# Rotary embedding on GpSimd cut into nine instructions, and two small steps moved, in an attention and gated-convolution kernel

## Chip, core and metric

The kernel runs on one core of one Trainium2 chip. The metric is device time in microseconds (us) for one execution, from launch to end; times stand as the median of three executions. The engines are TensorE (PE in the profile, with PEld for its weight loads), VectorE (DVE), ScalarE (ACT), GpSimd (POOL) and SyncE (SP), whose queue issues the DMAs here.

## Reference

Attention with a rotary embedding (rope) on q and k, then two matrix products with a three-tap convolution and a gate between them. All arrays are f32.

```python
batch, n_heads, seq, head_dim = 4, 8, 576, 64      # d_model 512, d_ff 1024
def rotate(x):                                      # half = 32
    x1, x2 = x[..., :half], x[..., half:]
    return concat([x1 * cos - x2 * sin, x1 * sin + x2 * cos])
scores = rotate(q) @ rotate(k).T / sqrt(64)
attn = softmax(scores)                              # row maximum subtracted
x = (attn @ v) laid out as (batch, seq, 512)
h = relu(x @ w_in)
c = conv_w[0] * h[t-1] + conv_w[1] * h[t] + conv_w[2] * h[t+1]
out = (h * sigmoid(c)) @ w_out
```

## The kernel before

The work on attention goes by pairs of heads, p = 0 to 15, with five score tiles each (`emit_S`, steps s = 0 to 4). A hand-written plan puts every piece into a numbered slot n with a rank; within a slot, pieces are emitted by rising rank, and each engine runs its instructions in the order of emission. Pair p has its score tiles in slots 5p to 5p+4. Up to slot 25 (`WIDE` is 26) the kernel does attention and turns the weights from 64-bit to f32 (`conv_w_piece`, lines 469 to 530); the text calls this the attention stage. From slot 26 on, the matrix products of the second part (`emit_M1`, `emit_M2`) are woven in between; this is the mixed stage. A tail runs the last two blocks of the second part alone.

For one score tile PE writes scores to PSUM (line 232), DVE takes the negated row maximum (`reds`, line 240), ACT takes the exponential with the row sum (`exps`, line 244), PE transposes the result (lines 289, 301 and 306), and ACT or DVE copies it out to `pt` (`evac`, lines 170 and 172). Two score tiles fit into PSUM, so PE's next scores wait for ACT's exponential to free one. `emit_Trem` makes the small transposes and their copies, and `emit_E` multiplies the probabilities by v (line 342); its last products read the small copies.

Rope of pair p runs on POOL (lines 163 and 164): one multiplication over 1152 columns in place, and one addition over 576 columns. It is emitted at the end of slot 5p-6 for q and 5p-5 for k. DVE turns the results by a 32x32 transpose into `qT` and `kT` (`emit_TQ`, lines 209 and 213) in slots 5p-4 and 5p-2. After the q transpose, ACT multiplies `qT` by the scale in place (line 210, recorded under the helper's line 170). That multiplication goes through `defer(k, ...)`: it is emitted k ticks later, a tick being one step of a piece on PE, of which a slot has some four to six.

`emit_rinv` (lines 315 and 316, DVE) adds a small number to the row sums and takes reciprocals; `emit_rinvT` a slot later turns them with PE and spreads them by DMA; `norm` uses them three slots after `emit_rinv`.

The second part's DVE work for one block of 128 features is lines 385 (multiply), 387 twice (multiply and add), and 396 (gate), all from SBUF; ACT and POOL split the result into two parts (lines 404 and 405). POOL also splits the normalized attention output (line 359).

Of the kernel before, what the change touches and what calls it, by code (L numbers as in the profile page):

```python
# [12 lines left out]
ALU = mybir.AluOpType  # L13
# [7 lines left out]
def attention_moe_kernel(ctx, tc, q, k, v, w_in, conv_w, w_out, tab, tabx, out):  # L21
    nc = tc.nc
# [12 lines left out]
    scale = float(D) ** -0.5  # L35
# [21 lines left out]
    tabt = keep.tile([128, S // 32, 2, 32], F32, name="tabt")  # L57
# [21 lines left out]
    def defer(k, fn, rank=1):  # L79
        due.setdefault(slot[0] + k, []).append((rank, len(due.get(slot[0] + k, [])), fn))  # L80
# [79 lines left out]

    def rope(p, part):
        x = raw[p, part]
        nc.gpsimd.tensor_tensor(out=x, in0=x, in1=tabt, op=ALU.mult)  # L163
        nc.gpsimd.tensor_tensor(out=x[:, :, 0, :], in0=x[:, :, 0, :], in1=x[:, :, 1, :], op=ALU.add)

    QT, KT = {}, {}

    def evac(eng, out, in_, sc=None):
        if eng == "A" or "m" not in psum:
            nc.scalar.activation(out=out, in_=in_, func=AF.Copy, scale=1.0 if sc is None else sc)  # L170
        elif sc is None:
            nc.vector.tensor_copy(out, in_)
        else:
            nc.vector.tensor_scalar(out=out, in0=in_, scalar1=sc, scalar2=None, op0=ALU.mult)

    def qk_tiles(p):
        if p not in QT:
            QT[p] = p2.tile([128, S], F32, tag="qT", name="qT")
            KT[p] = p2.tile([128, S + 64], F32, tag="kT", name="kT")

    def k_rem(p):
        if p * STEPS < WIDE:
            for h in range(2):
                r = slice(64 * h, 64 * h + 64)
                evac("V", krem[p % 2][r, r], KT[p][r, 576:640])
# [19 lines left out]
    def emit_TQ(p, part):  # L205
        qk_tiles(p)
        x = raw.pop((p, part))[:, :, 0, :]
        if part == "q":
            nc.vector.transpose(out=QT[p].rearrange("p (c i) -> p c i", i=32), in_=x)
            defer(1, lambda: evac("A", QT[p], QT[p], scale))  # L210
        else:
            kt = KT[p].rearrange("p (c i) -> p c i", i=32)
            nc.vector.transpose(out=kt[:, 2:20], in_=x)
            nc.vector.transpose(out=kt[:, 0:2], in_=x[:, 16:18])
            k_rem(p)
# [5 lines left out]
    def go(d, key):  # L221
        for fn in d.pop(key):
            fn()
# [58 lines left out]
    def emit_T(p, s, h=None):  # L282
        if p not in PT:
            PT[p] = ptp.tile([128, 9, S], F32, tag="pt", name="pt")
        pt = PT[p]
        ps = t_tile()
        st = STR[p] if s == 4 else ST[p, s][:, h, 64 * h:64 * h + 512]
        for t in range(4):
            nc.tensor.transpose(ps[:, 128 * t:128 * t + 128], st[:, 128 * t:128 * t + 128], idf)  # L289
        if s == 4:  # L290
            evac("A", pt[:, 0:8, 512:S], ps.rearrange("p (k c) -> p k c", k=8))
        else:
            evac("A", pt[:, h:8:2, 128 * s:128 * s + 128], ps.rearrange("p (k c) -> p k c", k=4))

    def emit_Trem(p, g):
        pt = PT[p]
        ps = t_tile()
        if g < 2:
            for u in range(2):
                x = ST[p, 2 * g + u].rearrange("p h k -> p (h k)")[:, 512:640]  # L300
                nc.tensor.transpose(ps[:, 128 * u:128 * u + 128], x, idf)
            evac("V", pt[:, 8, 256 * g:256 * g + 256], ps[:, 0:256])
        else:
            for h in range(2):
                x = strem[p % 2][:, 512 - 64 * h:640 - 64 * h]
                nc.tensor.transpose(ps[:, 128 * h:128 * h + 128], x, idf)
            for h in range(2):
                r = slice(64 * h, 64 * h + 64)
                evac("V", pt[r, 8, 512:S], ps[r, 192 * h:192 * h + 64])
# [3 lines left out]
    def emit_rinv(p):  # L313
        s = p % 2
        nc.vector.tensor_scalar(out=sums[p], in0=sums[p], scalar1=1e-9, scalar2=None, op0=ALU.add)
        nc.vector.reciprocal(out=rvc[s][:, 0:9], in_=sums[p])

    def emit_rinvT(p):
        s = p % 2
        ps = t_tile()[0:32, 0:128]  # L320
        nc.tensor.transpose(ps, rvc[s], idf)
        st = p1.tile([32, 128], F32, tag="rst", name="rst")
        evac("V", st, ps)
        d = scr.tile([9, 128], F32, tag="d", name="rd")
        nc.sync.dma_start(out=d, in_=st[0:9, :])
        fl = d.rearrange("(o t) n -> o (t n)", o=1)
        rbt = rb[p] = p1.tile([128, S], F32, tag="rb", name="rb")
        nc.sync.dma_start(out=rbt[0:64, :], in_=fl[:, 0:S].to_broadcast([64, S]))
        nc.sync.dma_start(out=rbt[64:128, 0:512], in_=fl[:, 640:1152].to_broadcast([64, 512]))
        nc.sync.dma_start(out=rbt[64:128, 512:S], in_=fl[:, 576:640].to_broadcast([64, 64]))  # L330
# [5 lines left out]
    def emit_E(p, j):  # L336
        b, hp = divmod(p, NPB)
        xp = t_tile()
        o = (S - XW) * j
        for i in range(5):  # L340
            for h in range(2):
                nc.tensor.matmul(  # L342
                    out=xp[64 * h:64 * h + 64, 0:XW],
                    lhsT=vmain[p][:, h, i, :] if i < 4 else vrem[:, h, :],
                    rhs=PT[p][:, 2 * i + h if i < 4 else 8, o:o + XW],
                    start=(i == 0),
                    stop=(i == 4),
                )
        xn = p2.tile([128, XW], F32, tag="xn", name="xn", bufs=3)
        nc.scalar.activation(out=xn, in_=xp[:, 0:XW], func=AF.Copy)  # L350

        def norm():
            sl = xslot[b, hp, j] = free_slots.pop(0)
            nc.vector.tensor_tensor(out=xn, in0=xn, in1=rb[p][:, o:o + XW], op=ALU.mult)

        def split():
            sl = xslot[b, hp, j]
            nc.scalar.activation(out=xT[:, sl, 0, :], in_=xn, func=AF.Copy)  # L358
            nc.gpsimd.tensor_tensor(out=xT[:, sl, 1, :], in0=xn, in1=xT[:, sl, 0, :].bitcast(F32), op=ALU.subtract)  # L359

        norms[p, j] = lambda: (norm(), defer(1, split))
# [208 lines left out]
    def at(n, rank, fn):  # L570
        plan.setdefault(n, []).append((rank, len(plan.get(n, [])), fn))

    def emit():
        with tc.manual_schedule(engines=engines):
# [17 lines left out]
            for p in range(1, NP):  # L592
                n = STEPS * p
                for i, part in enumerate("qk"):
                    if p > 1:
                        at(n - 9 + 2 * i, 19, lambda p=p, part=part: load(p, part))
                    at(max(n - 6 + i, 0) if p > 1 else 0, 18, lambda p=p, part=part: rope(p, part))
                    at(max(n - 4 + 2 * i, 2), 0.45, lambda p=p, part=part: emit_TQ(p, part))
                at(n + 1, 19, lambda p=p: load_v(p))
            for p in range(NP):  # L600
                n = STEPS * p
                for s in range(STEPS):
                    m = n + s
                    first = m < WIDE
                    if m:
                        at(m - 1 if first else m, 0.5 if first else 0, lambda p=p, s=s: emit_S(p, s))
                    at(m, 0.2, lambda p=p, s=s: go(reds, (p, s)))
                    at(m, 0.3 if first else 1.5, lambda p=p, s=s: go(exps, (p, s)))
                    for h in range(2 if s < 4 else 1):
                        at(m + 1, 0 if m + 1 < WIDE else 1, lambda p=p, s=s, h=h: emit_T(p, s, h))  # L610
                for g, e in ((0, 2), (1, 4), (2, 5)):
                    at(n + e, 2, lambda p=p, g=g: emit_Trem(p, g))
                at(n + 4, 4, lambda p=p: emit_E(p, 0))
                at(n + 5, 4, lambda p=p: emit_E(p, 1))
                at(n + 5, 1.7, lambda p=p: emit_rinv(p))
                at(n + 6, 2, lambda p=p: emit_rinvT(p))
                for j in range(2):
                    at(n + 8, 1.7 + j, lambda p=p, j=j: norms.pop((p, j))())
            nw = len(wsteps)
            for i, u in enumerate(wsteps):  # L620
                x = (WIDE - 1) * i // nw
# [66 lines left out]
            for u in seq + second + m2_units(last) + m2_units(LASTB):  # L688
                u()
                tick()  # L690

    emit()


# [47 lines left out]
```

## Time and profile before

| What | Value |
|---|---|
| Median of three executions | 581.32 us (576.83 to 585.36) |
| Profiled execution, its own time | 585.31 us |
| Span of the profiled execution, first to last instruction | 583.2 us |
| PE busy | 513.9 us, 88% of the span |
| DVE busy | 417.5 us, 72% |
| ACT busy | 316.6 us, 54% |
| POOL busy | 241.3 us, 41% |
| Granted TensorE clock, mean | 0.959 of full speed |

A busy share says how long an engine had something in it, also while that instruction waited inside the engine. The chain of waits ends last through PE for 58% of the span, through DVE for 21% and through ACT for 9%. What a stretch is worth is read from the idle time of PE in it and from who ended that idle time.

### The profile page before, as it was taken

To read this page: it belongs to the slowest core of one execution; us is meant where nothing else is said; L and a number is where in the kernel's file an instruction comes from. 1 tells how busy PE (TensorE), PEld (TensorE's weight loads), DVE (VectorE), ACT (ScalarE), POOL (GpSimd) and SP (SyncE) were. 2 spreads that over 40 slices of the span, in tenths; PEclk is the share of its full clock that TensorE was granted. 3 is DMA by queue.
4 is the path that set the end of the run, shared out by engine and by line. 5 is a ranking of instruction groups with operands and counts; after the bars stand their busy time and mean duration, and the time that the engine had idled before them with its cause. 6 is when DMAs were issued, how large, how long until landed. Compare 5 with 4: busy or idle time off the path is not lost.

```text
span 583.2 us, 9069 instructions
## 1 busy us (share of the span) xinstructions
PE 513.9 (88%) x3160; PEld 364.0 (62%) x3160; DVE 417.5 (72%) x668; ACT 316.6 (54%) x810; POOL 241.3 (41%) x221
## 2 busy tenths in 40 slices
PE   3597879788895999897998899997998999999997
PEld 1253434344664667674777577674866767779986
DVE  4888778784586958878598848877288847466971
ACT  2678676675654655565546545574255646334530
POOL 3636547554363534427071714545044212142440
PEclk9979989998896999999999989997999999999999
DMA  9774663934422315051513214060240101000001
GB/s 216 138 155 117 150 143 90 197 75 82 81 42 57 67 50 92 8 113 22 113 28 83 59 54 88 17 124 1 77 83 21 41 22 39 22 37 19 1 36 55
DMA packets 138385, 42.51 MB, mean 73 GB/s; under 512 B 131004, under 2 KB 131940, under 8 KB 138340
## 3 DMA queue, kind: packets, MB, share of 16 engines
q1 hardware_dynamic: 136996, 41.54, 32.6%
q8 instruction: 25, 0.41, 0.3%
q10 hardware_dynamic: 1344, 0.39, 0.3%
q14 instruction: 20, 0.16, 0.1%
HBM read 37.12 MB, written 4.79 MB: 72 GB/s over the span
## 4 chain that ended last, share of the span: by engine, by line
PE 58%; DVE 21%; ACT 9%; DMA 5%; issue 4%; SPq 3%; DVEq 0%; ACTq 0%
PE sp L232 12%; PE pm L451 9%; PE tp L342 8%; PE pm L373 8%; PE tp L289 8%; PE mt L451 6%; DVE c L387 5%; PE mt L373 4%; DVE negm L240 4%; DVE c L385 3%; ACT st L244 3%; DVE c L396 2%; ACT pt L170 2%; DMA w<-moe_w_in 1%; DMA rq<-q 1%
## 5 line engine op out<-in xcount | busy, mean ns | idle before, releaser
L170 ACT ACTIVATE pt<-tp 128x512 f32<-128x512 f32 (+2 forms) x164 | 86.3, 557 | 102.7 <-PE tp L289 98.4
L240 DVE TENSOR_REDUCE negm<-sp 128x1 f32<-128x576 f32 x144 | 102.7, 749 | 42.3 <-PE sp L232 41.8
L405 POOL TENSOR_TENSOR g<-c,g 128x288 fp32r<-128x288 f32 (+4 forms) x88 | 56.2, 650 | 169.9 <-ACT g L404 163.6
L232 PE MATMUL sp<-kT,qT 64*128 64x288 f32 (+4 forms) x556 | 111.3, 490 | 15.9 <-ACT st L244 15.9
L244 ACT ACTIVATE st<-sp,negm 128x576 f32<-128x576 f32 x128 | 93.4, 739 | 14.4 <-DVE negm L240 10.7
L387 DVE SCALAR_TENSOR_TENSOR c<-rr,cw,c 128x288 f32<-128x288 f32 x128 | 91.7, 717 | 4.5
L289 PE MATMUL tp<-idf,st 128*128 128x128 f32 x512 | 78.6, 294 | 17.8 <-ACT st L244 11.5
L289 PEld LDWEIGHTS tp<-idf,st 128*128 128x128 f32 x512 | 58.1, 147 | 47.2 <-ACT st L244 17.4
L373 PE MATMUL pm<-xT,winh 128*128 128x290 f32 x384 | 84.5, 312 | 0.5 <-ACT rr L381 0.5
L232 PEld LDWEIGHTS sp<-kT,qT 64*128 64x128 f32 (+1 forms) x556 | 49.5, 184 | 54.4 <-ACT st L244 25.0
L342 PE MATMUL tp<-pt,vm 128*64 128x290 f32 x512 | 71.7, 423 | 3.7 <-ACT pt L170 3.4
L359 POOL TENSOR_TENSOR xT<-xn,xT 128x290 fp32r<-128x290 f32 x32 | 27.5, 880 | 94.2 <-ACT xT L358 92.9
L373 PEld LDWEIGHTS pm<-xT,winh 128*128 128x128 f32 x384 | 62.8, 194 | 1.4 <-ACT rr L381 0.7
L451 PE MATMUL pm<-wouth,g 128*128 128x512 f32 x176 | 62.2, 411 | 0.0
L396 DVE SCALAR_TENSOR_TENSOR c<-c,rr 128x288 f32<-128x288 f32 x64 | 48.6, 759 | 16.8 <-ACT c L393 16.5
L385 DVE TENSOR_SCALAR c<-rr,cw 128x288 f32<-128x288 f32 x64 | 47.4, 741 | 14.8 <-ACT rr L381 14.5
L373 PE MATMUL pm<-xT,winl 128*128 128x290 f32 x192 | 57.5, 300 | 0.0
L342 PEld LDWEIGHTS tp<-pt,vm 128*64 128x64 f32 x512 | 34.7, 140 | 30.0 <-ACT pt L170 5.1
L163 POOL TENSOR_TENSOR rq<-rq,tabt 128x1152 f32<-128x1152 f32 x15 | 40.5, 2700 | 5.5 <-DMA rq<-q 5.5
L393 ACT ACTIVATE c<-c 128x288 f32<-128x288 f32 x64 | 28.4, 444 | 22.6 <-DVE c L387 22.3
L163 POOL TENSOR_TENSOR rk<-rk,tabt 128x1152 f32<-128x1152 f32 x15 | 40.5, 2701 | 0.0
L451 PEld LDWEIGHTS pm<-wouth,g 128*128 128x128 f32 x176 | 33.5, 190 | 9.7 <-issue 2.2
(99 smaller groups left out, 761.9 us busy)
## 6 DMA issues: line engine op xcount, KB each, us to landing
out<-ot SPq DMA_DIRECT2D x17, 256.0 KB, 2.1
rq<-q SPq DMA_DIRECT2D x30, 144.0 KB, 3.2
rq<-q SPq DMA_DIRECT2D x60, 72.0 KB, 2.9
rk<-k SPq DMA_DIRECT2D x30, 144.0 KB, 3.1
rk<-k SPq DMA_DIRECT2D x60, 72.0 KB, 2.9
w<-moe_w_in SPq DMA_DIRECT2D x8, 512.0 KB, 5.0
vm<-v SPq DMA_DIRECT2D x32, 128.0 KB, 2.5
w<-moe_w_out SPq DMA_DIRECT2D x8, 512.0 KB, 4.2
```

What stands on the lines that cost most here:

```text
L163: nc.gpsimd.tensor_tensor(out=x, in0=x, in1=tabt, op=ALU.mult)
L170: nc.scalar.activation(out=out, in_=in_, func=AF.Copy, scale=1.0 if sc is None else sc)
L232: nc.tensor.matmul(out=out, lhsT=qt[64 * h:64 * h + 64, c], rhs=kt[64 * h:64 * h + 64, a:a + n], start=True, stop=True)
L240: reds.setdefault((p, s), []).append(lambda: nc.vector.tensor_reduce(out=nm, in_=sc, axis=AX.XY if len(sc.shape) == 3 else AX.X, op=ALU.ma ...
L244: lambda: nc.scalar.activation(out=dst, in_=sc, func=AF.Exp, bias=nm, scale=1.0, accum_out=sm)
L289: nc.tensor.transpose(ps[:, 128 * t:128 * t + 128], st[:, 128 * t:128 * t + 128], idf)
L342: nc.tensor.matmul(out=xp[64 * h:64 * h + 64, 0:XW], lhsT=vmain[p][:, h, i, :] if i < 4 else vrem[:, h, :], rhs=PT[p][:, 2 * i + h if i < ...
L373: nc.tensor.matmul(out=ps[:, 0:XW], lhsT=w[:, kk, fs], rhs=xT[:, xs, e, :], start=(i == 0), stop=(i == n - 1))
L385: nc.vector.tensor_scalar(out=c, in0=r[:, j:j + HS], scalar1=cw[:, f:f + 1], scalar2=None, op0=ALU.mult)
L387: nc.vector.scalar_tensor_tensor(out=c, in0=r[:, j + e:j + e + HS], scalar=cw[:, 8 * e + f:8 * e + f + 1], in1=c, op0=ALU.mult, op1=ALU.add,)
L396: nc.vector.scalar_tensor_tensor(out=c, in0=c, scalar=1.0, in1=r[:, j + 1:j + 1 + HS], op0=ALU.add, op1=ALU.mult)
L451: nc.tensor.matmul(out=ops[tt][:, 0:width], lhsT=g_tile(tt, f, e), rhs=w[:, f, cols], start=(f == 0 and i == 0), stop=(f == NF - 1 and i = ...
```

## The change

Three edits. Rope of one tensor becomes nine POOL instructions of 192 columns (six multiplications, three additions) in place of two. The multiplication of q by the scale on ACT is deferred by five ticks in place of one. The sums and reciprocals of a pair move within their slot from rank 1.7 to rank 4.5, that is behind the small transposes with their copies (rank 2) and the second half of the product with v (rank 4).

```diff
     def rope(p, part):
         x = raw[p, part]
-        nc.gpsimd.tensor_tensor(out=x, in0=x, in1=tabt, op=ALU.mult)
-        nc.gpsimd.tensor_tensor(out=x[:, :, 0, :], in0=x[:, :, 0, :], in1=x[:, :, 1, :], op=ALU.add)
+        for a in range(0, 18, 3):
+            y = x[:, a:a + 3]
+            nc.gpsimd.tensor_tensor(out=y, in0=y, in1=tabt[:, a:a + 3], op=ALU.mult)
+        for a in range(0, 18, 6):
+            y = x[:, a:a + 6]
+            nc.gpsimd.tensor_tensor(out=y[:, :, 0, :], in0=y[:, :, 0, :], in1=y[:, :, 1, :], op=ALU.add)
@@
-            defer(1, lambda: evac("A", QT[p], QT[p], scale))
+            defer(5, lambda: evac("A", QT[p], QT[p], scale))
@@
-                at(n + 5, 1.7, lambda p=p: emit_rinv(p))
+                at(n + 5, 4.5, lambda p=p: emit_rinv(p))
```

## Rows read from the trace of the kernel before

**Rows 1.** Attention and mixed stage: us; busy PE, PEld, DVE, ACT, POOL; granted clock; DMA.

```profile
15.00:155.00 140.00, 111.33 (x620) 59.84 (x619) 106.28 (x155) 99.19 (x242) 79.10 (x56) 0.91 0.59 124
155.00:505.00 350.00, 324.61 (x2100) 236.54 (x2099) 255.00 (x408) 188.92 (x487) 133.77 (x120) 0.97 0.26 56
```

**Rows 2.** Who waited for whom, mixed stage: total us, times, longest.

```profile
PE sp L232 <- ACT st L244: 13.9, 11, 6.4
PE tp L342 <- DVE pt L172: 8.6, 4, 2.5
ACT qT L170 <- DVE qT L209: 8.5, 5, 1.7
```

**Rows 3.** DVE instructions by source line, ns min/median/max.

```profile
L385 DVE TENSOR_SCALAR c<-rr,cw x64: 356/370/2761, 156.1 to 560.5; 128x288 f32<-128x288 f32 x64
...
L387 DVE SCALAR_TENSOR_TENSOR c<-rr,cw,c x128: 517/520/2770, 156.5 to 561.5; 128x288 f32<-128x288 f32 x128
...
L315 DVE TENSOR_SCALAR sums<-sums x16: 157/166/2596, 39.3 to 497.4; 128x9 f32<-128x9 f32 x16
...
L240 DVE TENSOR_REDUCE negm<-sp x144: 698/748/759, 15.3 to 492.3; 128x1 f32<-128x576 f32 x144
```

**Rows 4.** One q rope and the DVE beside it, in order of time.

```profile
294.22 2.85 POOL L163 TENSOR_TENSOR rq<-rq,tabt 128x1152 f32<-128x1152 f32 x1
297.15 1.41 POOL L164 TENSOR_TENSOR rq<-rq 128x576 f32<-128x576 f32 x1
...
294.83 2.41 DVE L385 TENSOR_SCALAR c<-rr,cw 128x288 f32<-128x288 f32 x1
297.28 2.16 DVE L387 SCALAR_TENSOR_TENSOR c<-rr,cw,c 128x288 f32<-128x288 f32 x2
```

**Rows 5.** POOL durations: rope by source line (min/median/max), a split by shape (mean).

```profile
L163 POOL TENSOR_TENSOR rq<-rq,tabt x15: 2610/2635/3073, 16.6 to 431.8; 128x1152 f32<-128x1152 f32 x15
...
L164 POOL TENSOR_TENSOR rq<-rq x15: 1398/1462/1735, 19.3 to 434.7; 128x576 f32<-128x576 f32 x15
...
L405 POOL TENSOR_TENSOR g<-c,g 128x192 fp32r<-128x192 f32 x8 | 6.0, 751 | 0.0
```

**Rows 6.** Two queued POOL pieces with two DVE instructions arriving, in order of time.

```profile
247.42 1.15 POOL L405 TENSOR_TENSOR g<-c,g 128x224 fp32r<-128x224 f32 x2 [5.32 <-ACT g L404]
...
247.51 1.44 DVE L387 SCALAR_TENSOR_TENSOR c<-rr,cw,c 128x288 f32<-128x288 f32 x2
```

**Rows 7.** The scale of q between the maxima and the exponentials.

```profile
242.50 1.42 DVE L240 TENSOR_REDUCE negm<-sp 128x1 f32<-128x576 f32 x2
243.84 0.77 DVE L209 STREAM_TRANSPOSE qT<-rq 128x576 f32<-128x576 f32 x1
244.64 0.68 ACT L170 ACTIVATE qT<-qT 128x576 f32<-128x576 f32 x1 [1.69 <-DVE qT L209]
...
246.10 2.78 PE L232 MATMUL sp<-kT,qT 64*128 64x288 f32 x8 [1.62 <-ACT st L244]
```

**Rows 8.** The longest wait of PE in the mixed stage, and DVE ahead of it.

```profile
173.93 2.76 DVE L385 TENSOR_SCALAR c<-rr,cw 128x288 f32<-128x288 f32 x1
...
182.89 3.01 PE L232 MATMUL sp<-kT,qT 64*128 64x288 f32 x8 [6.35 <-ACT st L244]
```

**Rows 9.** Sums ahead of the small copies.

```profile
270.00 1.53 DVE L315 TENSOR_SCALAR sums<-sums 128x9 f32<-128x9 f32 x1
271.69 0.40 DVE L172 COPY pt<-tp 64x64 f32<-64x64 f32 x2
272.14 0.71 PE L342 MATMUL tp<-pt,vr 128*64 128x290 f32 x4 [2.51 <-DVE pt L172]
```

**Rows 10.** Attention stage: a q transpose on rope, and two long waits of PE.

```profile
28.15 0.69 PE L289 MATMUL tp<-idf,st 128*128 128x128 f32 x4 [3.83 <-ACT st L244]
...
46.20 0.78 DVE L209 STREAM_TRANSPOSE qT<-rq 128x576 f32<-128x576 f32 x1 [1.30 <-POOL rq L164]
...
149.31 1.96 PE L232 MATMUL sp<-kT,qT 64*128 64x288 f32 x8 [2.01 <-ACT st L244]
```

## Prediction

> **What bounds the kernel now.** I read busy time by stage first [rows 1]. In the mixed stage PE is busy 324.61 of 350 us, so 25.4 us are idle. The attention stage has 28.7 us of idle PE in 140; the tail I leave as it is. PE is the bound; a change that does not touch its work can give back its idle time and what the clock loses behind it, and no more. The waits of the mixed stage say who ended that idle time [rows 2]: ACT's exponential before new scores, 13.9 us, and the small DVE copies before the last products with v, 8.6 us. Together that is 22.5 of the 25.4. So I asked next what made those two late.
>
> Both come out of DVE's queue. By source line [rows 3], line 385 has a median of 370 ns and a maximum of 2761, line 387 520 and 2770, and line 315, which works on nine columns, 166 and 2596. The maximum reduction of line 240, which reads PSUM, stays between 698 and 759 ns. One rope beside DVE shows what the long ones are [rows 4]: POOL multiplies from 294.22 to 297.07, and line 385, begun at 294.83, ends at 297.24, when that is over; the pair of line 387 then takes 2.16 us, 1.12 above two medians, beside the addition that ends at 298.56. A DVE instruction on SBUF stands still until the POOL instruction under way has ended, and one of them gets in at the boundary. This trio lost 2.04 + 1.12 = 3.2 us, and every reduction queued behind it came so much later.
>
> **Part by part: rope in nine.** Rope's two lengths give the price of a piece [rows 5]: (2610 - 1398) / 576 columns = 2.10 ns per column, so 2610 - 1152 x 2.10 leaves some 0.19 us per instruction, and 192 columns cost 0.19 + 0.40 = 0.59 us. Nine make 5.3 us, where the medians of the two make 4.1: 1.2 us more per rope, 36 us over 30 ropes, on an engine busy 41% of the span. The upper bound is the 0.75 us mean of the 192-column split, which includes waiting: 6.8 us, 2.7 more. I take the lower value, since those two minima are undisturbed. In the mixed stage the cover is the slots between rope and transpose; if it were gone, the transpose and the reductions behind it on DVE would come 1.2 us later.
>
> What DVE gets back: an arriving instruction waits for the rest of one piece, on average 0.3 us, and the next ones, arriving as POOL has just gone on, between 0 and 0.59; I take 0.45. The trio then loses 1.2 us, not 3.2. On PE this counts only where PE waits. The longest wait, 6.35 us, has such a trio ahead of it, whose first instruction, line 385, took 2.76 us against a median of 0.37 [rows 8]; 2 us come back there. The rest of rope's gain in this stage, at the waits that the other two edits also shorten, I put at another 2 us: 4 in all, bounds 0 and 6.
>
> The GPSIMD Engine Reference of the Trainium skill (section 2.1, Instruction dispatch) says that a GpSimd core starts the next instruction when it has finished its own share, and that nothing holds it back. By that, nine queued multiplications need show no boundary at all; the rival on starvation below works out the same thing from rows.
>
> **The scale of q later.** In the mixed stage ACT waited for the q transpose five times, 8.5 us [rows 2]. Rows 7 show one [rows 7]: two maxima are taken from 242.50, the first is there by 243.2, but ACT has the scale ahead of the exponentials and waits for the transpose until 244.64; after its 0.68 us the first exponential follows, at some 245.2, and PE's scores wait 1.62 us for it. With five ticks the scale falls behind those exponentials, and its 0.68 us go to a place where the transpose is long done; ACT is busy 189 of 350 us [rows 1], which covers them, and the scores that read q follow three slots after the transpose. If it met another exponential head on, the cost would be 0.68 each. The exponentials can start 2.0 us earlier, more than the wait. Four such waits of PE, one to every second pair, are 1.6 each, the first of them shown [rows 7], and of the 6.35 one 1.7, ACT's wait, is this: 4 x 1.6 + 1.7 = 8.1 us.
>
> **Sums behind the copies.** Line 315 held DVE from 270.00 to 271.53, and the small copies began at 271.69; PE waited 2.51 us for them [rows 9]. Put behind, they start 1.7 us sooner. Three of the four waits are such (the first is shown), the fourth is what is left, 8.6 - 3 x 2.5 = 1.1, of which I count half: 3 x 1.7 + 0.5 = 5.6 us, bounds 0 and 8.6. What is queued behind the moved pair on DVE is the convolution and the next maxima; with pieces they lose up to 0.59 us there, hidden as long as PE has products of the second part to do. The PE transpose of the reciprocals comes a slot later, so nobody waits for them at once. In the tail of the plan the last pair's sums start behind PE's work too, for which I count nothing.
>
> **Clock.** In the mixed stage the granted clock is 0.97 [rows 1], so 350 x 0.03 = 10.5 us of full speed are missing. That is a mean over the two levels, 1.2 and 2.4 GHz. I suppose, without a row that proves it, that the lower one stands behind PE's idle stretches; with three quarters of these gone I take half back, 5 us, bounds 0 and 10.5.
>
> **Attention stage.** Three effects of about 2 us or more. The 3.83 us wait at 28.15 stands behind weight conversion held by the first ropes, and the 2.01 us wait at 149.31 behind a scale [rows 10]: I count 3 and 2 us back. Against it, one q transpose already waited 1.30 us for rope [rows 10]; a rope that is 1.2 us longer, or 2.4 for the second of two in a row, moves it and the maxima behind it. I set 3 us against, bounds 0 and 9. Net 2 us faster, from 6 faster to 4 slower. The idle time there that is due to weight transfers stays.
>
> **Sum.** 8.1 + 5.6 + 4 + 5 + 2 = 24.7 us off the profiled execution's 585.31: 560.6. The profiled execution is 0.7% over the median of 581.32; scaled by 581.32 / 585.31 the forecast is 557 us. All 22.5 us of waits, the whole clock and 6 us of the attention stage are 39 us: 542.6. Scale and sums alone, with 4 us lost in attention, are 9.7: 571.7.
>
> **Rivals.** *A new wait takes the old one's place.* Rope now lasts 5.3 us and more with DVE in between, so more DVE instructions fall into it, each paying up to 0.59; the reductions stay late, and ACT waits for them where it waited for the scale. For it: seven DVE instructions on SBUF in a row would lose as much as now, 7 x 0.45. Against it: runs before a reduction are of three or four, and reductions and PSUM copies do not wait at all [rows 3]. Only the 8.1 us remain: 577.2, or 573 by the median.
>
> *Starvation, the slower side.* If POOL goes from piece to piece without letting DVE in, a trio that arrives 0.6 us into rope loses 4.7 us at once, 1.6 more than now. At some 13 of the 18 ropes of the mixed stage (pairs 7 to 15, two each) that is 21 us later for PE; more idle time costs the clock again what it costs now, 10 us; scale and sums give 13.7 back. Net 17 slower: 602, or 598 by the median. It decides once most boundaries stay shut. Against it stands a pair of queued POOL pieces with two DVE instructions arriving [rows 6]: these took 1.44 us, 0.4 over their medians, where waiting out both pieces would have cost 0.9 or more. The SBUF — State Buffer page of the Trainium skill (Who interferes with whom) has the port pair held for a whole instruction and issue order deciding who blocks; rows 4 agree on the first, with 2.41 us for line 385.
>
> *The change does not do what it says:* five ticks put the scale ahead of another exponential that waits as long, and the freed DVE time was hidden: no change, 581.
>
> **How the numbers follow.** Forecast 0.70, new wait 0.20, starvation 0.05, no effect 0.05. The measurement of this kernel tells 2% from no change; 2% below the median is 569.7. Nine tenths of the forecast's chance, and a third of the new wait's with its own spread, lie below that: 0.70 faster by over 2%; slower by over 2% is starvation and a little of what I don't see, 0.06; the rest, 0.24, within. The range runs from 542 to 577: the bounds of the forecast, and most of the new wait; starvation, no effect and the ends are left out, under 0.2.
>
> **What the profile would show.** Right: pieces near 0.6 us, maxima of lines 385 and 387 near 1.1 us; no wait of ACT for the q transpose in the mixed stage; the two waits of PE down from 22.5 us to some 6; a clock of 0.98 or more there. Starvation would leave DVE maxima near 5 us. A new wait would show as ACT waiting for the reductions while the scale waits no more. I would be wrong if PE's idle time returned behind DVE transposes that wait for rope.

## The result, and the profile after

The changed kernel takes 546.58 us against 580.86 beside it: 0.941 of the time, 95% interval 0.933 to 0.948, 34 us or 5.9% faster. A second set of runs gave 0.942 (0.938 to 0.947). The forecast was 557 with a range of 542 to 577: faster, as forecast, and by 10 us more.

In the changed file every line behind rope stands four lines further down: the reduction is line 244, the exponential 248, the convolution 389, 391 and 400, the scale and the other copies on ACT 174, the sums 319, POOL's split 409.

The page after, its busy times, its slices and its granted clock:

```profile
span 546.1 us, 9285 instructions
...
PE 501.0 (92%) x3160; PEld 356.3 (65%) x3160; DVE 374.4 (69%) x668; ACT 314.2 (58%) x810; POOL 283.8 (52%) x431
...
PE   2788869787899999999999999999999999999997
...
PEclk9989896989999999999999999999999999999999
...
PE 70%; ACT 8%; DVE 8%; DMA 6%; POOL 2%; issue 2%; SPq 2%; ACTq 0%; DVEq 0%; POOLq 0%
```

DVE's busy time fell by 43 us with not one instruction fewer (668 in both), POOL's rose by 42. On the chain that ends last DVE went from 21% to 8%, and PE from 58% to 70%. In the slices PE is at nine from the twelfth to the last but one.

The mixed stage is best cut by its own marks, from the first product of the second part to the first of the tail. Windows of the kernel before, then of the one after:

```profile
152.50:512.80 360.30, 334.40 (x2155) 245.64 (x2155) 260.20 (x418) 193.67 (x500) 136.19 (x124) 0.96 0.26 56
```

```profile
148.50:476.20 327.70, 322.00 (x2156) 238.69 (x2155) 228.46 (x420) 192.75 (x502) 163.75 (x262) 1.00 0.29 62
```

The columns are those of [rows 1]. The same products take 32.6 us less: PE's idle time went from 25.9 to 5.7 us, and its busy time from 334.4 to 322.0 at a clock of 1.00, which was 0.96. The stretch ahead of the mark is 4 us shorter, the tail half a microsecond.

DVE's and POOL's instructions by source line after (ns, min/median/max), which answer to [rows 3, 5]:

```profile
L165 POOL TENSOR_TENSOR rq<-rq,tabt x90: 581/596/1042, 16.7 to 401.3; 128x192 f32<-128x192 f32 x90
...
L168 POOL TENSOR_TENSOR rq<-rq x45: 580/589/1038, 20.2 to 403.0; 128x192 f32<-128x192 f32 x45
...
L389 DVE TENSOR_SCALAR c<-rr,cw x64: 355/370/982, 151.9 to 523.5; 128x288 f32<-128x288 f32 x64
...
L391 DVE SCALAR_TENSOR_TENSOR c<-rr,cw,c x128: 517/521/1169, 152.3 to 524.5; 128x288 f32<-128x288 f32 x128
...
L319 DVE TENSOR_SCALAR sums<-sums x16: 164/555/758, 36.9 to 465.4; 128x9 f32<-128x9 f32 x16
```

A piece is 0.59 us, as worked out. The longest instruction of the convolution fell from 2770 to 1169 ns, 0.65 over its median: one piece. The median of the sums rose from 166 to 555; presumably they now stand beside a piece of rope more often, which no run separates. In this profile no engine waited for them.

What became of the waits in the mixed stage, after, answering to [rows 2]:

```profile
PE tp L346 <- ACT pt L174: 2.8, 6, 0.5
...
PE sp L236 <- ACT st L248: 2.4, 9, 0.5
```

PE's wait for the exponentials fell from 13.9 to 2.4 us, that for the small DVE copies is gone, and ACT waits for the q transpose no more. The stretch of the longest wait, 6.35 us before [rows 8], reads so after, in order of time on ACT and PE:

```profile
171.67 0.74 ACT L248 ACTIVATE st<-sp,negm 128x576 f32<-128x576 f32 x1
...
175.97 0.67 ACT L174 ACTIVATE qT<-qT 128x576 f32<-128x576 f32 x1
```

```profile
172.56 1.96 PE L236 MATMUL sp<-kT,qT 64*128 64x288 f32 x8 [0.44 <-ACT st L248]
```

The exponential comes first, the scale 4 us later, and PE waits 0.44 us.

### The profile page after: what moved, and what is told of

It is laid out like the page before. It is cut to its first block, busy times and chain, and to the rows that moved or that the text cites. A ratio compares the mean times of both kernels' runs of the same rounds, so it can differ in the third digit from the quotient of the medians.

```text
span 546.1 us, 9285 instructions
## 1 busy us (share of the span) xinstructions
PE 501.0 (92%) x3160; PEld 356.3 (65%) x3160; DVE 374.4 (69%) x668; ACT 314.2 (58%) x810; POOL 283.8 (52%) x431
## 4 chain that ended last, share of the span: by engine, by line
PE 70%; ACT 8%; DVE 8%; DMA 6%; POOL 2%; issue 2%; SPq 2%; ACTq 0%; DVEq 0%; POOLq 0%
PE sp L236 14%; PE tp L346 13%; PE pm L455 11%; PE pm L377 10%; PE tp L293 9%; PE mt L455 6%; PE mt L377 5%; ACT pt L174 3%; ACT st L248 3%; DVE negm L244 2%; POOL rq L165 2%; DMA rq<-q 2%; DMA w<-moe_w_out 1%; DVE c L391 1%; DMA rb<-rd 1%
## 5 line engine op out<-in xcount | busy, mean ns | idle before, releaser
L236 PE MATMUL sp<-kT,qT 64*128 64x288 f32 (+4 forms) x556 | 106.0, 475 | 3.3 <-ACT st L248 3.3
L293 PE MATMUL tp<-idf,st 128*128 128x128 f32 x512 | 74.7, 283 | 15.4 <-ACT st L248 9.0
L391 DVE SCALAR_TENSOR_TENSOR c<-rr,cw,c 128x288 f32<-128x288 f32 x128 | 83.1, 649 | 4.5
L377 PE MATMUL pm<-xT,winh 128*128 128x290 f32 x384 | 82.8, 308 | 0.5 <-ACT rr L385 0.5
L293 PEld LDWEIGHTS tp<-idf,st 128*128 128x128 f32 x512 | 54.8, 141 | 43.0 <-ACT st L248 14.6
L236 PEld LDWEIGHTS sp<-kT,qT 64*128 64x128 f32 (+1 forms) x556 | 46.6, 177 | 38.8 <-issue 16.4
L165 POOL TENSOR_TENSOR rq<-rq,tabt 128x192 f32<-128x192 f32 x90 | 58.7, 685 | 5.6 <-DMA rq<-q 5.6
L165 POOL TENSOR_TENSOR rk<-rk,tabt 128x192 f32<-128x192 f32 x90 | 57.6, 672 | 0.0
L400 DVE SCALAR_TENSOR_TENSOR c<-c,rr 128x288 f32<-128x288 f32 x64 | 40.3, 630 | 17.2 <-ACT c L397 17.0
L354 ACT ACTIVATE xn<-tp 128x290 f32<-128x290 f32 x32 | 13.2, 413 | 46.9 <-PE tp L346 43.2
```

The source lines that it names most:

```text
L165: nc.gpsimd.tensor_tensor(out=y, in0=y, in1=tabt[:, a:a + 3], op=ALU.mult)
L236: nc.tensor.matmul(out=out, lhsT=qt[64 * h:64 * h + 64, c], rhs=kt[64 * h:64 * h + 64, a:a + n], start=True, stop=True)
L377: nc.tensor.matmul(out=ps[:, 0:XW], lhsT=w[:, kk, fs], rhs=xT[:, xs, e, :], start=(i == 0), stop=(i == n - 1))
L391: nc.vector.scalar_tensor_tensor(out=c, in0=r[:, j + e:j + e + HS], scalar=cw[:, 8 * e + f:8 * e + f + 1], in1=c, op0=ALU.mult, op1=ALU.add,)
L400: nc.vector.scalar_tensor_tensor(out=c, in0=c, scalar=1.0, in1=r[:, j + 1:j + 1 + HS], op0=ALU.add, op1=ALU.mult)
```

## Experiments

Twelve runs, each as a ratio to the kernel before on the same chip. The theory of the forecast was that the three edits add. The rival that came up on seeing the result was one cause: blocked DVE instructions make the reductions, the q transpose and the small copies late together, and rope in pieces cures all of it.

**One edit alone, and two without rope.**

```diff
# e1_rope: the first hunk of the change alone
# e2_scale: defer(1, ...) -> defer(5, ...) alone
# e3_sums: rank 1.7 -> 4.5 alone
# e4_scale_sums: the second and third hunk, rope in two instructions
```

> Only rope in nine instructions; scale and sums stay where they were. If the three edits add as in the forecast, this gives rope's 4 us, the 3 us of the attention stage and a third of the clock, some 9 us off the kernel before: about 572. If the blocked DVE is the one cause of all the late steps (one-cause theory), the maxima, the q transpose and the small copies all come early enough without moving anything, and 25 us or more go: about 555 or less, with ACT waiting for the q transpose as long as before but PE no longer waiting behind it.

> Only the deferral of the scale by five ticks. If the edits add: 8.1 us in the mixed stage, 2 in the attention stage and some 2 us of clock, 12 off: about 569. One-cause theory: the exponentials still stand behind late maxima, so only part of each 1.6 us wait goes, 6 us off or less: about 575.

> Only the sums behind the small copies. If the edits add: 5.6 us and one of clock, about 574. One-cause theory: the copies come earlier, but the sums, now beside the same long rope, hold the convolution and the next maxima instead, and 3 us or less go: about 578.

> The changed kernel with rope in two instructions again, so scale and sums without rope. If the edits add: 8.1 + 5.6 us, 2 in the attention stage and 3 of clock, 19 off: about 562. One-cause theory: about 570 or more, with PE's waits for the exponentials still some 8 us in the mixed stage.

| Kernel | Median, us | Ratio (95% interval) |
|---|---|---|
| rope in nine alone | 549.46 | 0.950 (0.946 to 0.955) |
| scale later alone | 570.20 | 0.985 (0.979 to 0.990) |
| sums later alone | 574.20 | 0.990 (0.987 to 0.993) |
| scale and sums, rope in two | 564.68 | 0.976 (0.971 to 0.981) |

Rope alone gives 31.7 us. Scale alone gives 10.9 and sums alone 6.9, close to the 12 and 7 that the terms had for them, and both together 16.4: these two nearly add. But the three singles add to 49.5 where the whole change gives 34.3: they remove the same waits. With rope alone, the mixed stage shows

```profile
PE sp L236 <- ACT st L248: 2.5, 7, 1.3
...
PEld tp L346 <- DVE pt L176: 0.4, 1, 0.4
...
ACT qT L174 <- DVE qT L213: 0.2, 1, 0.2
```

though scale and sums stand where they stood. ACT's 8.5 us of waiting for the q transpose [rows 2] had come from the queue ahead of the transpose on DVE, not from the place of the scale. The one-cause theory holds for rope, though not in all it said: I had expected ACT to wait for the q transpose as long as before. Its forecasts for scale and sums alone (575 and 578) were too pessimistic, since each also removes those waits from its own end. In the mixed stage with scale alone, then with sums alone, PE waits so, where it waited 13.9 and 8.6 us before [rows 2]:

```profile
PE sp L232 <- ACT st L244: 5.9, 8, 4.5
```

```profile
PE tp L342 <- DVE pt L172: 2.2, 4, 0.9
```

**What the two small edits add to rope.** The changed kernel with one of them undone, and the changed kernel beside it.

```diff
# e5_rope_scale: at(n + 5, 4.5, ... emit_rinv) -> 1.7 again
# e6_rope_sums: defer(5, ...) -> defer(1, ...) again
# e12_again: the changed kernel
```

> The changed kernel with the sums back ahead of the small copies, so rope in nine and the later scale. Rope alone gave 0.950 of the kernel before, all three 0.941. One-cause theory: with short pieces the sums cost the copies 0.6 us at most, four times, so putting them back loses 0 to 2 us against the changed kernel run beside it. If the sums' own 5.6 us stand by themselves, 5 us or more are lost.

> The changed kernel with the scale of q one tick behind the transpose again, so rope in nine and the later sums. One-cause theory: in the mixed stage nothing is lost, and in the attention stage, where the q transpose waits for rope on DVE, ACT stands behind the scale for as long: 2 to 4 us slower than the changed kernel beside it. If the scale's own 8.1 us stand by themselves, 8 us or more.

> The changed kernel itself once more, as the measure for the three beside it: 0.941 of the kernel before, 546 to 548.

Medians: 547.81 (0.942, 0.938 to 0.946), 554.04 (0.952, 0.948 to 0.956), and 549.00 for the changed kernel (0.942, 0.938 to 0.947). The sums are worth nothing on top of rope; the scale 5 us, which lies between the two forecasts, and not where expected. I had expected no loss in the mixed stage, but without the deferral it takes 334.0 us, 6.3 more than in the changed kernel. ACT waited there five times for the q transpose, 3.6 us in all, with the scale ahead of the exponentials. Once, at 172 us, PE waited 2.06 us for scores behind it. Windows of the kernel without the deferral, then of the changed kernel at the same place:

```profile
165.00:175.00 10.00, 7.95 (x57) 5.62 (x56) 6.80 (x13) 6.25 (x18) 9.14 (x15) 0.97 0.00 1
175.00:185.00 10.00, 10.00 (x54) 8.36 (x53) 5.51 (x11) 5.19 (x14) 0.80 (x1) 0.69 0.57 120
```

```profile
165.00:175.00 10.00, 9.56 (x67) 6.45 (x67) 8.19 (x16) 5.71 (x17) 8.97 (x14) 1.00 0.01 1
175.00:185.00 10.00, 9.25 (x65) 7.22 (x64) 7.71 (x16) 8.58 (x22) 2.17 (x3) 1.00 0.61 135
```

Behind the wait the granted clock is 0.69 for ten microseconds, with PE busy throughout: at the lower of its two levels for about six of the ten, by estimate some 3 us of work lost behind 2 us of idling. The other four times the wait shows inside PE's scores. ACT and PE without the deferral at one of them, then PE's same scores in the second profile of the changed kernel:

```profile
233.54 0.69 ACT L174 ACTIVATE qT<-qT 128x576 f32<-128x576 f32 x1 [0.74 <-DVE qT L213]
...
235.00 1.96 PE L236 MATMUL sp<-kT,qT 64*128 64x288 f32 x8 [0.15 <-ACT st L248]
```

```profile
232.47 1.24 PE L236 MATMUL sp<-kT,qT 64*128 64x288 f32 x8
```

That is 0.7 us longer, and it comes four times, at one pair in two: 2.9 of the 6.3 us. So a part of the 1.6 us each that the forecast had counted for the scale stays with it even beside rope in nine.

**Other lengths of the pieces, and no rope.**

```diff
# e8_coarse, three instructions of 576 columns:
-        for a in range(0, 18, 3):          # y = x[:, a:a + 3]
+        for a in range(0, 18, 9):          # y = x[:, a:a + 9]
-        for a in range(0, 18, 6):          # y = x[:, a:a + 6]
+        for a in range(0, 18, 18):         # y = x[:, a:a + 18]
# e11_mid, 14 instructions of 128: steps 2 and 4
# e7_fine, 27 instructions of 64: steps 1 and 2
# e9_no_rope:
+        nc.gpsimd.tensor_tensor(out=x[:, 0:1], in0=x[:, 0:1], in1=tabt[:, 0:1], op=ALU.mult)   # and nothing else
```

> The changed kernel with rope in three instructions of 576 columns. A piece takes some 1.4 us, a rope 4.2. Piece-length theory: DVE's longest waits are about 1.2 us, and the time lies between two instructions (565, scale and sums moved) and nine (547): about 553. Rival (only the 2.6 us multiplication hurts, any cut of it is enough): 547 or, with the shorter rope, less.

> The changed kernel with rope in 14 instructions, nine multiplications and five additions, of 128 columns (the last addition 64). By 0.19 us and 2.10 ns per column 0.46 us a piece, 6.3 us a rope, one more than with nine. If 64 columns lost by starvation, DVE passing over several boundaries, and this begins only below some length, 128 columns may stay free of it: DVE's maxima near 1 us, 547 to 550. If starvation grows as pieces get shorter, maxima of 2 us or more and 555 to 570. If 64 columns lost by rope's length alone (POOL late), 14 pieces lose a quarter of it: about 558, with DVE's maxima near 1 us.

> The changed kernel with rope in 27 instructions of 64 columns (18 multiplications, 9 additions). At 0.19 us each and 2.10 ns per column that is some 0.32 us a piece and 8.8 us a rope, 3.4 more than with nine. Piece-length theory (what counts is how long one POOL instruction holds DVE): the mixed stage stays as it is with nine, since there the rope has slots to spare, and the attention stage loses 3 to 6 us on q transposes that wait for rope: about 551. Rival (more boundaries, more blocked DVE instructions, the new wait of the forecast): PE's waits return in the mixed stage, 558 or more.

> The changed kernel with rope left out but for one POOL instruction of 64 columns per tensor, so that the rotation of pairs 1 to 15 is not done. It is the floor: what rope in nine still costs. Piece-length theory: the mixed stage has 5 us of idle PE left, so nearly nothing comes back there, and the attention stage gives 3 to 5 us: about 543. If blocked DVE instructions still set the time, 535 or less.

| Rope (scale and sums later in all) | Median, us | Ratio (95% interval) |
|---|---|---|
| two, 1152 and 576 columns | 564.68 | 0.976 (0.971 to 0.981) |
| three of 576 | 565.17 | 0.973 (0.967 to 0.979) |
| nine of 192 | 546.58 | 0.941 (0.933 to 0.948) |
| 14 of 128 | 555.10 | 0.954 (0.950 to 0.957) |
| 27 of 64 | 592.15 | 1.019 (1.012 to 1.026) |
| left out but for one instruction of 64 columns per tensor | 546.12 | 0.938 (0.931 to 0.946) |

Nine is as fast as no rope at all, within the intervals: the mixed stage takes 327.8 us without rope and 327.7 with it in nine, so what rope still costs DVE there is wholly hidden. Both expectations on either side of nine failed.

Three pieces gain nothing. The rows of a k rope in three, POOL and DVE in order of time:

```profile
234.91 3.00 POOL L165 TENSOR_TENSOR rk<-rk,tabt 128x576 f32<-128x576 f32 x2
237.99 1.40 POOL L168 TENSOR_TENSOR rk<-rk 128x576 f32<-128x576 f32 x1
...
235.35 1.29 DVE L400 SCALAR_TENSOR_TENSOR c<-c,rr 128x288 f32<-128x288 f32 x1
236.57 1.50 DVE L389 TENSOR_SCALAR c<-rr,cw 128x288 f32<-128x288 f32 x1
238.11 2.44 DVE L391 SCALAR_TENSOR_TENSOR c<-rr,cw,c 128x288 f32<-128x288 f32 x2
```

Against medians of 0.46, 0.37 and 2 x 0.52 these lose 0.8 + 1.1 + 1.4 = 3.3 us, as much as the trio of [rows 4] lost with two. Each instruction of a run waits for up to one piece, so a run can lose its number of instructions times the piece, at most the rope. With three or four in a run, three pieces use up most of the rope as two did. I had interpolated in the length of a piece; the count belongs in it. DVE's busy time in the mixed stage says the same: 260.68 us with two (scale and sums later), 258.61 with three, 228.46 with nine and 212.73 with rope left out. Over the 18 ropes of that stage, DVE is held for about 2.7, 2.5 and 0.9 us per rope. Rope runs on beside reductions and PSUM copies, which don't wait.

Pieces of 64 are slower than the kernel before. Their POOL and DVE rows at one q rope:

```profile
217.47 2.53 POOL L168 TENSOR_TENSOR rq<-rq 128x64 f32<-128x64 f32 x9
219.96 0.82 POOL L409 TENSOR_TENSOR g<-c,g 128x288 fp32r<-128x288 f32 x1
...
217.36 4.10 DVE L400 SCALAR_TENSOR_TENSOR c<-c,rr 128x288 f32<-128x288 f32 x1 [0.96 <-ACT c L397]
```

The gate instruction, 0.46 us by itself, arrives at 217.36 and ends at 221.46: its wait ended at about 221.0, past the last of those additions and past the split that followed them, so it let nine boundaries go by. This is the rival of starvation. Six of line 400 took 2 us or more, up to 4.34, where the changed kernel's longest takes 1.06. And the rope is 8.6 us long: PE now waits for POOL's late splits, and DVE for rope ahead of its transposes, rows of the whole run:

```profile
DVE qT L213 <- POOL rq L168: 19.7, 5, 6.3
...
PE pm L455 <- POOL g L409: 11.5, 4, 3.8
...
DVE kT L217 <- POOL rk L168: 11.0, 5, 5.2
```

So 64 columns lose both ways. The first product of the second part starts 18 us later than with nine, at 166.7, and the mixed stage takes 353.2 us, 25.5 more. In the attention stage, from 15 to 150 us, rope on POOL has 62.7% of the chain that ends last, so there its length leads. In the mixed stage I cannot say how the loss divides: starved DVE instructions and late POOL stand in the same stretches.

At 128 columns the mixed stage is again as short as with nine (328.0 us, of which PE is idle for 5.6), and DVE's convolution stays at 1.17 us at most. The loss is in the attention stage, where one conversion of weights starved, 5.10 us where its median is 0.58:

```profile
48.96 3.75 POOL L165 TENSOR_TENSOR rk<-rk,tabt 128x128 f32<-128x128 f32 x9
52.68 1.96 POOL L168 TENSOR_TENSOR rk<-rk 128x128 f32<-128x128 f32 x5
...
51.04 5.10 DVE L476 TENSOR_SCALAR wt<-wt 128x512 f32<-128x512 f32 x1
```

The maxima behind it came late and PE's scores with them. This is the outcome that the expectation gave for starvation (555 to 570, with a maximum of 2 us or more), though in one instruction alone. The starvation theory is shown at 64 columns and, once, at 128; at 192 DVE missed no more than about one boundary, 1.38 us for a conversion of 0.43 (1.52 in the second profile of the changed kernel). Whether a boundary opens seems to depend on more than length: which DVE instruction waits may matter. No run separates that.

**Rope of q earlier.**

```diff
-                    at(max(n - 6 + i, 0) if p > 1 else 0, 18, ... rope(p, part))
+                    at(max(n - 7 + 2 * i, 0) if p > 1 else 0, 18, ... rope(p, part))
```

> The changed kernel with the rope of q one slot earlier (end of slot 5p-7 in place of 5p-6). In the changed kernel DVE waited three times for rope ahead of a q transpose, 6.9 us in all, in the attention stage. If these waits are on the path, they go and 3 to 5 us with them: about 542. If DVE's waiting is covered there by the weight transfers, nothing changes: 546.5, or a little more if the earlier rope waits for q's loads and holds POOL.

548.12 us, 0.943 (0.937 to 0.949): nothing. DVE's 6.9 us of waiting for rope ahead of the q transpose went away, but POOL now waits 28.2 us for q's loads there, in six ropes, and PE's time stays. The wait was covered in the attention stage, as the second theory had it. With rope left out altogether that stage is 2.9 us shorter, where I had expected 3 to 5: the first product of the second part starts at 145.71, where it starts at 148.56 in the changed kernel. These are single executions, and a second one of the changed kernel has 149.57, so about one microsecond may be chance.

## Why the forecast was right, and where its sizes were off

*What bounds the kernel.* Right: the idle time of PE in the mixed stage and the clock behind it were what could come back, and most of it did (20.2 of 25.9 us of idle time, and the clock). The view that decided was who ended PE's idle time, then the spread of durations by source line on DVE.

*Rope in nine.* The price of a piece was right (0.59 forecast, 0.593 measured), and so was the view that POOL's extra time (36 us forecast, 42 measured) would be covered. The gain was the mis-sized term: 4 us, or 9 with its share of the clock and the attention stage, where rope alone gave 31.7. The failing step is the sentence that set the rest of rope's gain "at the waits that the other two edits also shorten" at 2 us. I had given those waits to the edit that stands next to them in the queue, scale or sums, and left rope the remainder. Rows 4 already held the other reading: whatever stands behind a trio on DVE comes 2 us sooner, and every one of those waits was shorter than 2.6 us, but for the one of 6.35. With rope alone 2.5 us of PE's wait for the exponentials are left, the longest of them 1.3, and none of its wait for the small copies.

*Scale and sums.* Their terms, 8.1 and 5.6, were right for each edit alone: scale alone gave 10.9 with the attention stage and clock, where 12 had been worked out, sums alone 6.9 of 7. On top of rope the scale gives 5 and the sums nothing. The terms counted separately what rope alone removes. That hardly moved the sum: in the mixed stage the three terms of waits make 8.1 + 5.6 + 4 = 17.7 us, and 20.2 us of PE's idle time came back. That the total came near although its division among the edits was wrong is partly luck: what was too much for scale and sums stood in for what was too little for rope. The span fell by 37.1 us where the sum has 24.7. Of the 12.4 us between them, 7.4 are PE's busy time in the mixed stage, which the sum has under the clock, 2.5 the waits and 2 the attention stage.

*Clock.* 5 us forecast; in the mixed stage PE's busy time fell by 12.4 us for the same instructions, at a clock of 1.00 in place of 0.96. A part of the 12.4 is not the clock: PE's scores also get shorter when they wait less inside, as at 232.47 above. With one wait of 2.06 us put back, ten microseconds at 0.69 came back with it, so an idle stretch can bring the lower level, as supposed, and halving the recovery was needless: with the long waits gone, the whole stage runs at 1.00. But not every such stretch brings it. Behind the 2.51 us wait of [rows 9], which ends at 272.14, the kernel before goes on at full clock:

```profile
265.00:275.00 10.00, 7.03 (x53) 4.27 (x52) 9.09 (x13) 4.03 (x11) 7.10 (x6) 1.00 0.00 1
275.00:285.00 10.00, 10.00 (x58) 8.03 (x57) 3.74 (x7) 5.78 (x16) 0.95 (x2) 1.00 0.31 85
```

What decides between the two, no run here separates.

*Attention stage.* 2 us forecast, 4 measured (3 in the second profile of the changed kernel), inside its bounds.

*Rivals.* A new wait in place of the old did not appear at nine. Starvation did not either, as rows 6 had it, but it is real: below 192 columns it set in, and at 64 the kernel is 1.9% slower than before, with a DVE maximum of 4.34 us, near the 5 that the rival gave as its sign. By the GPSIMD Engine Reference of the Trainium skill (section 2.1, Instruction dispatch) a GpSimd core goes on to the next instruction without a barrier. What the prediction concluded from it, that no boundary need open, agrees with the 4.10 us beside nine short additions, and not with what happens at 192; the runs decide, and put the turn between 64 and 192 columns here, with one case at 128. By the SBUF — State Buffer page of the Trainium skill (Who interferes with whom) the later comer blocks for a whole instruction. That about holds for 192 columns and more: 0.65 us lost at most by the convolution beside pieces of 0.59, and in rows 4 a wait that ended with the multiplication.

The prediction's sentence that a DVE instruction on SBUF stands still until POOL's has ended is too wide: the q transpose at 46.20 [rows 10] reads and writes SBUF, and takes 0.78 us, where the longest and the shortest of the kernel's thirty differ by 0.01, though POOL multiplies from 46.12 to 48.75:

```profile
46.12 2.63 POOL L163 TENSOR_TENSOR rk<-rk,tabt 128x1152 f32<-128x1152 f32 x1
```

The instructions seen waiting here are, above all, those of the convolution, the sums and the weight conversion.

## What to carry to other kernels

When several late steps stand in one engine's queue, ask what makes that queue late before pricing each step: terms that remove the same wait don't add, and the edit at the root takes most. If GpSimd and VectorE work in SBUF side by side, cut the GpSimd instruction until the runs of VectorE instructions between two urgent ones lose little (number times piece), and stop before the pieces are so short that VectorE no longer gets in between: here nine of 192 columns were as good as no rope at all, three of 576 as bad as two, and 27 of 64 worse than two. When a wait of TensorE is priced, read the granted clock behind it too: here 2.06 us of waiting cost, by estimate, some 3 us more that way, and another wait, of 2.51 us, cost nothing more.

## What the runs showed of the hardware that was not expected

- A VectorE instruction that waits for GpSimd got in at about the next boundary between GpSimd instructions of 192 columns or more (at most 0.65 us over its median in the convolution, 1.1 over the shortest in the weight conversion), but passed over many boundaries between short ones: 4.10 us beside nine additions of 64 columns, 5.10 us once beside instructions of 128.
- The profile counts that waiting as busy time of VectorE: 43 us of its busy time went with no instruction fewer.
- Not every VectorE instruction on SBUF waits: a transpose took 0.78 us inside a GpSimd multiplication of 2.63 us.
- One idle stretch of 2.06 us on TensorE was followed by ten microseconds at a mean granted clock of 0.69, with TensorE busy throughout; one of 2.51 us was followed by full clock.
- A GpSimd instruction on two f32 inputs costs about 0.18 us and 2.1 ns per column: medians of 0.318 us for 64, 0.456 for 128, 0.593 for 192 and 1.41 for 576 columns.
